# One tile shape for the attention slot's last matmuls, and a planner that counts changes of tile shape

## The chip, the cores and the metric

The kernel runs on one core of one Trainium2 chip. The metric is device time in microseconds (us) of one execution. The kernel before takes 1174.6 us, the median of three runs (1174.29 to 1176.4). The engines are named as the profile names them: PE (TensorE: matmuls; PEld is its weight load), ACT (ScalarE), DVE (VectorE), POOL (GpSimd) and SP (SyncE, which here issues the DMAs). They work at the same time, each through its own list of instructions in order, and wait for each other by semaphores.

## The reference

A masked attention feeds two feed-forward layers. All data are float32.

```
scores = q @ k^T / 8                       # 4 batches x 8 heads, 576 x 576, head size 64
scores = where(scores >= rowmax - tau, scores, -1e9)
attn   = exp(scores - rowmax);  attn = attn / (sum(attn) + 1e-9)
x      = attn @ v                          # heads side by side: 2304 tokens x 512
g  = softplus(x @ w_in);    x = g @ w_out       # layer 1, 512 -> 2048 -> 512
g  = relu(x2 @ w2_in)**2;   out = g @ w2_out    # layer 2, x2 is layer 1's output
```

## The kernel before, in words

**Attention** is cut into 32 units: a group of 288 queries (eight groups, two for each batch) times a pair of heads (four). A unit's scores stand transposed, keys on the 128 partitions and 288 queries along the row. 576 keys are four chunks of 128 and one of 64 for each head; the two 64-key rests of the two heads share the ninth slot of the tile `st` (128 x 9 x 288), head 0's in partitions 0 to 63 and head 1's in 64 to 127. That is the shared slot.

For each unit `a_scores` makes the scores: four chunk pieces (L364), each two matmuls that use 64 of the array's 128 rows, one per head, and a piece for the shared slot (L369). The first eight units multiply in float32; the others split k and q into a high and a low part and make three faster products. ACT copies each result to `st` (L372). `a_max` and `a_soft` take maximum, subtract, mask (DVE, L379 to L405) and exponential (ACT, L406). `a_out` multiplies by v and sums the weights, both in float32: X (head 0 in partitions 0 to 63 of the bank `a_ps0`, head 1 in 64 to 127) takes eight matmuls of 128 rows and 64 columns (L420), D (the sums, in `a_ps1`, head 0 in the upper and head 1 in the lower half) takes eight of 128 rows by the 32 columns of a tile of ones (L427), and the shared slot adds four matmuls to them: X and D for head 0, X and D for head 1 (L432, L433, L432, L433), with 64 rows, and 64 columns for X and 32 for D. ACT copies X and D out, DVE divides.

**Layer 1** has eight groups of 288 tokens and eight steps per group, 64 steps in all: `m1_up` (L463 to L465, three products for the split operands), softplus (ACT L473 to L475, DVE L476), split (`m1_split`: ACT L481, DVE or POOL L482), `m1_down` (L494 to L496). Weights are loaded, split into high and low parts by ACT, DVE and POOL, and stay in SBUF. **Layer 2** follows with five groups of tokens.

**The order** of the instructions on each engine is made by a planner, `Plan`. Every piece of work is added with an engine, a duration in ns, what it reads and writes, and a key (a due time). `emit` schedules them forward in a list simulation, turns the result into new keys by a backward pass, repeats this for 24 rounds, and emits the shortest of the orders. It is called twice: for all attention units with most of layer 1, and for the rest. The banks `a_ps0` and `a_ps1` hold both a unit's scores (from the seventh unit on) and X and D, so that a score piece can start only when ACT has copied the last one out.

Of the kernel before, what the change touches and what calls it, by code (L numbers as in the profile page):

```python
# [2 lines left out]

# [6 lines left out]
F32 = mybir.dt.float32  # L10
# [3 lines left out]
ALU = mybir.AluOpType  # L14
AX = mybir.AxisListType

B, H, S, D = 4, 8, 576, 64
# [9 lines left out]
LAG = 12  # L27
# [10 lines left out]
def f32(ap):  # L38
    return ap.bitcast(F32)


class Plan:
# [3 lines left out]

    SYNC, AFTER_PE, DRAIN, DMA_START, DMA_END, BYTES_PER_NS = 200, 300, 130, 1600, 950, 300

    def __init__(self):
        self.ops, self.writer, self.readers = [], {}, {}
        self.free, self.bus, self.done, self.lock = {}, 0, [], 0

    def add(self, eng, ns, fn, reads=(), writes=(), key=0.0, nbytes=0, lock=False):
        i = len(self.ops)
        deps = set()
        for r in reads:
            if r in self.writer:
                deps.add(self.writer[r])  # L60
            self.readers.setdefault(r, []).append(i)
        for w in writes:
            if w in self.writer:
                deps.add(self.writer[w])
            deps.update(self.readers.pop(w, ()))
            self.writer[w] = i
        deps.discard(i)
        self.ops.append((eng, ns, fn, deps, key, nbytes, lock or eng == "POOL"))

    def emit(self, rounds=24):  # L70

        first, n = len(self.done), len(self.ops)
        state = self.free, self.bus, self.lock
        self.done += [None] * (n - first)
        users = [[] for _ in range(n - first)]
        for i in range(first, n):  # L80
            for d in self.ops[i][3]:
                if d >= first:
                    users[d - first].append(i)
        keys = [op[4] for op in self.ops[first:]]
        best = None
        for r in range(rounds):
            self.free, self.bus, self.lock = dict(state[0]), *state[1:]
            order = self.forward(first, users, keys)
            length = max(self.free.values())
            if best is None or length < best[0]:  # L90
                best = length, order, self.done[first:], (self.free, self.bus, self.lock)
            keys = self.backward(first, users, order)
        _, order, self.done[first:], (self.free, self.bus, self.lock) = best
        for _, _, i in order:
            self.ops[i][2]()

    def forward(self, first, users, keys):
        n = len(self.ops)
        waits = [0] * (n - first)
        ready_at = [0] * (n - first)  # L100
        for i in range(first, n):
            for d in self.ops[i][3]:
                if d < first:
                    ready_at[i - first] = max(ready_at[i - first], self.seen(d, self.ops[i][0]))
                else:
                    waits[i - first] += 1
        engines = sorted({op[0] for op in self.ops[first:]})
        future, ready = {e: [] for e in engines}, {e: [] for e in engines}
        for e in engines:
            self.free.setdefault(e, 0)  # L110

        def release(i):
            heapq.heappush(future[self.ops[i][0]], (ready_at[i - first], keys[i - first], i))

        for i in range(first, n):
            if not waits[i - first]:
                release(i)
        order = []
        while len(order) < n - first:
            best = None  # L120
            for e in engines:
                t = self.free[e]
                if not ready[e] and future[e]:
                    t = max(t, future[e][0][0])
                elif not ready[e]:
                    continue
                if best is None or t < best[0]:
                    best = (t, e)
            t, e = best
            while future[e] and future[e][0][0] <= t:  # L130
                _, key, i = heapq.heappop(future[e])
                heapq.heappush(ready[e], (key, i))
            _, i = heapq.heappop(ready[e])
            eng, ns, fn, deps, key, nbytes, lock = self.ops[i]
            if lock:
                t = max(t, self.lock)
                self.lock = t + ns
            self.free[e] = end = t + ns
            if nbytes:
                self.bus = max(self.bus, t + self.DMA_START) + nbytes / self.BYTES_PER_NS  # L140
                end = self.bus + self.DMA_END
            self.done[i] = (end, e)
            order.append((t, len(order), i))
            for u in users[i - first]:
                ready_at[u - first] = max(ready_at[u - first], self.seen(i, self.ops[u][0]))
                waits[u - first] -= 1
                if not waits[u - first]:
                    release(u)
        return sorted(order)

    def backward(self, first, users, order):
# [18 lines left out]
        while left:  # L170
# [11 lines left out]
                _, key, i = heapq.heappop(future[e])  # L182
                heapq.heappush(ready[e], (key, i))
            _, i = heapq.heappop(ready[e])
            eng, ns, fn, deps, key, nbytes, lock = self.ops[i]
            if lock:
                t = max(t, lock_at)
                lock_at = t + ns
# [29 lines left out]
def kernel(ctx: ExitStack, tc: tile.TileContext, qT, kT, vp, tau, w1i, w1o, w2i, w2o, out):  # L218
# [55 lines left out]
    NX = 5  # L274
    xf_t = many(NX, [128, HALF], "xf")
    w_t = ap.tile([128, 18], F32, name="w_t")
    one_t = ap.tile([128, 32], F32, name="one_t")
    POOL.memset(one_t, 1.0)
    m_d = [dram.tile([18, 32], F32, name=f"m_d{i}") for i in range(4)]


# [4 lines left out]
    class Weights:  # L286
# [7 lines left out]
        def load(self, src, f, outw, key=None, pe=False):  # L294
# [19 lines left out]
            if pe:  # L314
# [6 lines left out]
                b2 = bank if outw else bank.rearrange("p (k f) -> p k f", k=4)  # L321
                P.add("ACT", 530, lambda: ACT.copy(lf, b2), [BK], [W], key)
                return
            P.add("POOL", 1240, lambda: POOL.tensor_tensor(lf, f32(t2), f32(hf), op=ALU.subtract), [T], [W], key)


    def a_load(u, key):
# [10 lines left out]
    def a_prep(u, key):  # L338
        if u < RAW:
            return  # L340
        k_r, q_r, KR, QR = k_rt[u % 2], q_rt[u % 2], ("k_r", u % 2), ("q_r", u % 2)
        P.add("ACT", 330, lambda: ACT.copy(q_h, q_r), [QR], ["q_h"], key)
        P.add("ACT", 630, lambda: ACT.copy(k_h, k_r), [KR], ["k_h"], key)
        P.add("POOL", 750, lambda: POOL.tensor_tensor(q_l, q_r, f32(q_h), op=ALU.subtract), [QR, "q_h"], ["q_l"], key)
        P.add("POOL", 1520, lambda: POOL.tensor_tensor(k_l, k_r, f32(k_h), op=ALU.subtract), [KR, "k_h"], ["k_l"], key)

    def a_scores(u, key):

# [2 lines left out]
        half = [slice(0, 64), slice(64, 128)]  # L351
        ops = [(k_h, q_h), (k_l, q_h), (k_h, q_l)]
        QK = ["k_h", "k_l", "q_h", "q_l"]
        last, ns = 2, [590, 400]
        if u < RAW:
            ops, QK, last, ns = [(k_rt[u % 2], q_rt[u % 2])], [("k_r", u % 2), ("q_r", u % 2)], 0, [590, 590]
        for c in range(5):
            banks = [(y_ps[i], ("y", i)) for i in (2 * (c % 2), 2 * (c % 2) + 1)] if u < EARLY else [(a_ps[i], ("a", i)) for i in range(2)]
            cs = slice(128 * c, 128 * c + 128)
            if c < 4:  # L360
                def mms(banks=banks, cs=cs):
                    for n, (k, q) in enumerate(ops):
                        for o in range(2):
                            PE.matmul(banks[o][0][:, :HALF], k[half[o], cs], q[half[o]], start=(n == 0), stop=(n == last))  # L364
                P.add("PE", ns[0] * cold, mms, QK, [b[1] for b in banks], key + 0.1 * c)
            else:
                def mms(bank=banks[0][0], cs=cs):
                    for n, (k, q) in enumerate(ops):
                        PE.matmul(bank[:, :HALF], k[:, cs], q, start=(n == 0), stop=(n == last))  # L369
                P.add("PE", ns[1] * cold, mms, QK, [banks[0][1]], key + 0.1 * c)  # L370
# [37 lines left out]
    def a_out(u, key):  # L408
# [8 lines left out]
        for c in range(4):  # L417
            def mms(c=c):
                for o in range(2):
                    PE.matmul(X[64 * o:64 * o + 64], vt[:, 256 * o + 64 * c:256 * o + 64 * c + 64], e[:, 5 * o + c], start=(c == 0), stop=False)  # L420
            P.add("PE", (490 + 100 * (c == 0)) * cold, mms, E + [V], [AX0], key)
        for c in range(0, 4, 2):
            def mms(c=c):
                for o in range(2):
                    for i in range(2):
                        a = 64 - 64 * o + 32 * i
                        PE.matmul(D[a:a + 32], one_t, e[:, 5 * o + c + i], start=(c == 0), stop=(c == 2 and i == 1))  # L427
            P.add("PE", (490 + 100 * (c == 0)) * cold, mms, E, [AD], key)

        def mms():  # L430
            for o, h in enumerate(half):
                PE.matmul(X[h], vt[h, 512:], e[h, 4], start=False, stop=True)  # L432
                PE.matmul(D[64 - 64 * o:96 - 64 * o], one_t[h], e[h, 4], start=False, stop=True)  # L433
        P.add("PE", 590 * cold, mms, [E[0], V], [AX0, AD], key)
        P.add("ACT", 310, lambda: ACT.copy(xf, X), [AX0], [XF], key - 0.5)
        for o in range(2):
            P.add("ACT", 310, lambda o=o: ACT.copy(rb[half[o]], D[half[1 - o]]), [AD], [RB], key - 0.5)
# [38 lines left out]
            P.add("DVE", 370, lambda j=j, h=h, a=a: DVE.scalar_tensor_tensor(out=gt_t[j], in0=h, scalar=0.0, in1=a, op0=ALU.max, op1=ALU.add), [("h", j), A], [("gt", j)], key - 0.2)  # L476

    def m1_split(key):
        eng, e, ns = ("POOL", POOL, 750) if key - LAG in GPOOL else ("DVE", DVE, 375)
        for j in range(2):  # L480
            P.add("ACT", 330, lambda j=j: ACT.copy(g_hl[0][j], gt_t[j]), [("gt", j)], [("g_h", j)], key - 0.2)  # L481
            P.add(eng, ns, lambda j=j: e.tensor_tensor(g_hl[1][j], gt_t[j], f32(g_hl[0][j]), op=ALU.subtract), [("gt", j), ("g_h", j)], [("g_l", j)], key - 0.2, lock=True)  # L482
# [211 lines left out]
```

## Time and profile before

| | us |
|---|---|
| median of three runs | 1174.6 |
| profiled execution | 1177.02 |
| its span, first to last instruction | 1175.2 |
| PE busy, share of the span | 1145.8 (98%) |
| DVE busy | 698.6 (59%) |
| ACT busy | 690.8 (59%) |
| POOL busy | 245.6 (21%) |

The span is measured from the first instruction to the last; the 1.8 us between it and the time of that execution lie around it. Busy shares are means over stages that differ: DVE is at 96% of the stretch from 59 to 118 us and at 28% of the last 352 us. Where a row gives "x2" or "x16" that many matmuls are merged into one row; a float32 matmul of the program stands as two MATMUL records in the trace. A tile shape such as 64*32 is rows times columns of the array. A matmul's modelled end lies after the start of the next one, since they are pipelined, so the time of a piece is read from start to start.

### The profile page before, as it was taken

What the parts mean: (1) busy time and instruction counts of PE and PEld (TensorE: products, weight loads), DVE (VectorE), ACT (ScalarE), POOL (GpSimd) and SP (SyncE); (2) the same over time, 40 slices, a digit from 0 to 9 for tenths busy, and PEclk for the clock granted to TensorE, in tenths of its full rate; (3) what the DMA queues carried; (4) which work ended last, traced back from release to release, by engine and by line L of the source; (5) the groups of instructions that cost most, each with busy time, mean ns of one, the idle gap of its engine ahead of it and who ended that gap; (6) DMA issues with size and microseconds to landing.
All of it is one profiled execution on the core that took longest, in us unless ns stands there. A gap on an engine that the chain in (4) does not pass through costs nothing.

```text
span 1175.2 us, 18185 instructions
## 1 busy us (share of the span) xinstructions
PE 1145.8 (98%) x6992; PEld 887.8 (76%) x6992; DVE 698.6 (59%) x992; ACT 690.8 (59%) x1640; POOL 245.6 (21%) x209
## 2 busy tenths in 40 slices
PE   7779999999999999999999999999999999999998
PEld 3335777877877877877777879988888888888887
DVE  5999986766776666657656745889322322222232
ACT  6787887777777776777677657865322222222222
POOL 1024223332332232333223211444000000000000
PEclk9888999999999999999999999999999999999999
DMA  5365422112112112112111004765010010000010
GB/s 190 109 200 181 140 89 84 46 44 81 46 39 83 41 45 83 39 48 74 47 48 42 31 11 146 212 205 159 7 66 1 1 54 1 1 37 1 1 37 19
DMA packets 39291, 81.85 MB, mean 70 GB/s; under 512 B 6180, under 2 KB 14884, under 8 KB 39204
## 3 DMA queue, kind: packets, MB, share of 16 engines
q1 hardware_dynamic: 39204, 80.69, 21.6%
q8 instruction: 55, 0.90, 0.3%
q14 instruction: 32, 0.26, 0.1%
HBM read 71.17 MB, written 9.50 MB: 69 GB/s over the span
## 4 chain that ended last, share of the span: by engine, by line
PE 90%; DVE 4%; ACT 3%; DMA 1%; issue 0%; SPq 0%; ACTq 0%; DVEq 0%
PE h_ps L463 12%; PE h_ps L464 11%; PE h_ps L465 11%; PE y_ps L494 6%; PE y_ps L604 6%; PE y_ps L603 6%; PE y_ps L605 6%; PE y_ps L496 5%; PE y_ps L495 5%; PE a_ps L364 5%; PE a_ps L420 5%; PE a_ps L432 3%; PE a_ps L433 3%; PE a_ps L427 3%; DVE st L402 1%; PE a_ps L369 1%
## 5 line engine op out<-in xcount | busy, mean ns | idle before, releaser
L482 POOL TENSOR_TENSOR g_l<-gt,g_h 128x288 fp32r<-128x288 f32 x96 | 102.8, 1074 | 316.4 <-ACT g_h L481 278.8
L463 PE MATMUL h_ps<-x_h,wih 128*128 128x288 f32 x512 | 160.1, 313 | 0.7 <-DVE gt L476 0.7
L494 PE MATMUL y_ps<-g_h,woh 128*128 128x288 f32 x512 | 158.2, 309 | 0.0
L464 PE MATMUL h_ps<-x_l,wih 128*128 128x288 f32 x512 | 150.5, 294 | 1.2 <-DVE x_l L454 1.2
L465 PE MATMUL h_ps<-x_h,wil 128*128 128x288 f32 x512 | 151.6, 296 | 0.0
L496 PE MATMUL y_ps<-g_l,woh 128*128 128x288 f32 x512 | 151.1, 295 | 0.0
L495 PE MATMUL y_ps<-g_h,wol 128*128 128x288 f32 x512 | 150.9, 295 | 0.0
L402 DVE TENSOR_TENSOR st<-st,mb 64x288 f32<-64x288 f32 (+1 forms) x128 | 129.0, 1022 | 3.3 <-DMA mb<-m_d 2.2
L583 ACT ACTIVATE r<-h_ps 128x512 f32<-128x512 f32 (+1 forms) x80 | 44.5, 556 | 146.2 <-PE h_ps L465 145.8
L584 DVE SCALAR_TENSOR_TENSOR r<-h_ps,r 128x512 f32<-128x512 f32 (+1 forms) x80 | 51.0, 638 | 131.8 <-ACT r L583 131.6
L464 PE MATMUL h_ps<-y_l,wih 128*128 128x512 f32 (+1 forms) x320 | 120.1, 375 | 0.1
L590 ACT CAST g_h<-r 128x512 fp32r<-128x512 f32 (+1 forms) x80 | 46.2, 578 | 125.4 <-PE y_ps L604 125.4
L463 PE MATMUL h_ps<-y_h,wih 128*128 128x512 f32 (+1 forms) x320 | 119.2, 372 | 0.0
L465 PE MATMUL h_ps<-y_h,wil 128*128 128x512 f32 (+1 forms) x320 | 118.7, 371 | 0.0
L591 DVE TENSOR_TENSOR g_l<-r,g_h 128x512 fp32r<-128x512 f32 (+1 forms) x80 | 51.7, 646 | 110.9 <-ACT g_h L590 110.8
L604 PE MATMUL y_ps<-wol,g_h 128*128 128x512 f32 x288 | 114.1, 396 | 0.0
L603 PE MATMUL y_ps<-woh,g_h 128*128 128x512 f32 x288 | 114.1, 396 | 0.0
L605 PE MATMUL y_ps<-woh,g_l 128*128 128x512 f32 x288 | 114.0, 396 | 0.0
L463 PEld LDWEIGHTS h_ps<-x_h,wih 128*128 128x128 f32 x512 | 96.4, 188 | 21.9 <-issue 18.7
L494 PEld LDWEIGHTS y_ps<-g_h,woh 128*128 128x128 f32 x512 | 96.4, 188 | 16.4 <-issue 15.3
L405 DVE SCALAR_TENSOR_TENSOR st<-st,thr 128x1152 f32<-128x1152 f32 (+1 forms) x64 | 104.1, 1628 | 0.1
L476 DVE SCALAR_TENSOR_TENSOR gt<-h_ps,a_t 128x288 f32<-128x288 f32 x128 | 57.4, 450 | 77.3 <-ACT a_t L475 73.9
(102 smaller groups left out, 2410.5 us busy)
## 6 DMA issues: line engine op xcount, KB each, us to landing
k_r<-in_kT SPq DMA_DIRECT2D x32, 320.0 KB
v_t<-in_vp SPq DMA_DIRECT2D x32, 288.0 KB
wraw<-in_w1i SPq DMA_DIRECT2D x16, 512.0 KB
wraw<-in_w1o SPq DMA_DIRECT2D x16, 512.0 KB
wraw<-in_w2i SPq DMA_DIRECT2D x16, 512.0 KB
wraw<-in_w2o SPq DMA_DIRECT2D x16, 512.0 KB
mb<-m_d SPq DMA_DIRECT2D x28, 288.0 KB
q_r<-in_qT SPq DMA_DIRECT2D x32, 144.0 KB
```

Of the source, the lines that this page charges most:

```text
L402: DVE.tensor_tensor(st[p0:p1, a:a + n], st[p0:p1, a:a + n], mb[p0:p1, o:o + 1].to_broadcast([p1 - p0, n, HALF]), op=ALU.subtract),
L405: P.add("DVE", 315 * (s1 - s0), lambda x=x: DVE.scalar_tensor_tensor(out=x, in0=x, scalar=thr, in1=x, op0=ALU.is_lt, op1=ALU.subtract), [] ...
L463: PE.matmul(bank, wih[p][:, c, f], xh[c], start=(c == 0), stop=False)
L464: PE.matmul(bank, wih[p][:, c, f], xl[c], start=False, stop=False)
L465: PE.matmul(bank, wil[p][:, c, f], xh[c], start=False, stop=(c == 3))
L482: P.add(eng, ns, lambda j=j: e.tensor_tensor(g_hl[1][j], gt_t[j], f32(g_hl[0][j]), op=ALU.subtract), [("gt", j), ("g_h", j)], [("g_l", j)] ...
L494: PE.matmul(o, woh[p][:, j, es], g_h[j], start=first, stop=False)
L495: PE.matmul(o, wol[p][:, j, es], g_h[j], start=False, stop=False)
L496: PE.matmul(o, woh[p][:, j, es], g_l[j], start=False, stop=last)
L603: PE.matmul(o, g_h[j][:, ts], woh[p][:, j], start=first, stop=False)
L604: PE.matmul(o, g_h[j][:, ts], wol[p][:, j], start=False, stop=False)
L605: PE.matmul(o, g_l[j][:, ts], woh[p][:, j], start=False, stop=last)
```

## The change

First, the shared slot's four matmuls in `a_out` get one tile shape. The tile of ones grows from 32 to 64 columns, the second half zero, and D's two matmuls use all 64: four tiles of 64 rows by 64 columns, each in its own quarter of the array. D's earlier matmuls keep 32 columns and no longer carry the stop flag. Second, the planner gets a `mode` for each piece on PE (0 is the full array, 1 the chunk scores, 2 X, 3 D, 4 the shared slot), adds 105 ns where the mode changes, and takes a ready piece of the mode that PE is in when its key is within 1000 ns of the first one's. Durations are restated (the shared slot 484 ns where it had 590, chunk scores 393 where they had 590, POOL's subtractions longer). Third, `emit` runs 150 rounds, and every eighth round starts from the best order so far with random shifts of the keys.

```diff
+    SWITCH, NEAR = 105, 1000
-    def emit(self, rounds=24):
+    def emit(self, rounds=150):
-        best = None
+        best, rnd = None, random.Random(1)
...
-            keys = self.backward(first, users, order)
+            keys = self.backward(first, users, order if r % 8 else best[1])
+            if r % 8 == 0 and r:
+                keys = [k + rnd.gauss(0, 1500) for k in keys]
...
-            _, i = heapq.heappop(ready[e])
-            eng, ns, fn, deps, key, nbytes, lock = self.ops[i]
+            key, i = ready[e][0]
+            if e == "PE" and self.ops[i][7] != tiles:
+                key, i = min((r for r in ready[e] if r[0] < key + self.NEAR and self.ops[r[1]][7] == tiles), default=(key, i))
+            ready[e].remove((key, i))
+            heapq.heapify(ready[e])
+            eng, ns, fn, deps, key, nbytes, lock, mode = self.ops[i]
+            if e == "PE" and mode != tiles:
+                ns, tiles = ns + self.SWITCH, mode
...
-    one_t = ap.tile([128, 32], F32, name="one_t")
-    POOL.memset(one_t, 1.0)
+    one_t = ap.tile([128, 64], F32, name="one_t")
+    POOL.memset(one_t, 0.0)
+    POOL.memset(one_t[:, :32], 1.0)
...
-            P.add("POOL", 1240, lambda: POOL.tensor_tensor(lf, f32(t2), f32(hf), op=ALU.subtract), [T], [W], key)
+            P.add("POOL", 1500, lambda: POOL.tensor_tensor(lf, f32(t2), f32(hf), op=ALU.subtract), [T], [W], key)
...
-        last, ns = 2, [590, 400]
+        last, ns = 2, [393, 400]
...
-                        PE.matmul(D[a:a + 32], one_t, e[:, 5 * o + c + i], start=(c == 0), stop=(c == 2 and i == 1))
-            P.add("PE", (490 + 100 * (c == 0)) * cold, mms, E, [AD], key)
+                        PE.matmul(D[a:a + 32], one_t[:, :32], e[:, 5 * o + c + i], start=(c == 0), stop=False)
+            P.add("PE", 484 * cold, mms, E, [AD], key, mode=3)
...
                 PE.matmul(X[h], vt[h, 512:], e[h, 4], start=False, stop=True)
-                PE.matmul(D[64 - 64 * o:96 - 64 * o], one_t[h], e[h, 4], start=False, stop=True)
-        P.add("PE", 590 * cold, mms, [E[0], V], [AX0, AD], key)
+                PE.matmul(D[64 - 64 * o:128 - 64 * o], one_t[h], e[h, 4], start=False, stop=True)
+        P.add("PE", 484 * cold, mms, [E[0], V], [AX0, AD], key, mode=4)
```

All line numbers from L325 on move up by 11 in the changed kernel: L432 and L433 become L443 and L444. What stands on PE at the end of one unit's `a_out`, in the middle of layer 1, before (the two numbers after a name are the tile's own; 32x288 is the output's shape):

```order
L369 MATMUL a_ps_145<-q_l,k_h 128x288
L427 MATMUL a_ps_146<-st_158,one_t 32x288 x8
L420 MATMUL a_ps_145<-st_158,v_t_148 64x288 x8
L432 MATMUL a_ps_145<-st_158,v_t_148 64x288
L433 MATMUL a_ps_146<-st_158,one_t 32x288
L432 MATMUL a_ps_145<-st_158,v_t_148 64x288
L433 MATMUL a_ps_146<-st_158,one_t 32x288
L463 MATMUL h_ps_67<-x_h_125,wih_76 128x288
```

And now, on PE at a like place:

```order
L380 MATMUL a_ps_145<-q_l,k_h 128x288
L438 MATMUL a_ps_146<-st_158,one_t 32x288 x8
L431 MATMUL a_ps_145<-st_158,v_t_148 64x288 x8
L443 MATMUL a_ps_145<-st_158,v_t_148 64x288
L444 MATMUL a_ps_146<-st_158,one_t 64x288
L443 MATMUL a_ps_145<-st_158,v_t_148 64x288
L444 MATMUL a_ps_146<-st_158,one_t 64x288
L505 MATMUL y_ps_63<-g_h_131,woh_90 128x288
```

The order of the slot's four matmuls is the same; D's two are 64 wide now. Over the whole program PE's list holds 464 runs of equal tile shape before and 372 now, so 463 and 371 changes of shape. The slot alone had 96 changes inside it (three in each of 32 units) and has none now; everything else together has 367 before and 371 now.

On PE, two score pieces of one unit with layer 1's matmuls between them, at one of the shortest distances before (nine matmuls; 18 places have nine or eight):

```order
L364 MATMUL a_ps_145<-q_l,k_h 128x288
L364 MATMUL a_ps_146<-q_l,k_h 128x288
L494 MATMUL y_ps_64<-g_h_132,woh_91 128x288
L495 MATMUL y_ps_64<-g_h_132,wol_99 128x288
L496 MATMUL y_ps_64<-g_l_134,woh_91 128x288
L494 MATMUL y_ps_65<-g_h_132,woh_91 128x288
L495 MATMUL y_ps_65<-g_h_132,wol_99 128x288
L496 MATMUL y_ps_65<-g_l_134,woh_91 128x288
L494 MATMUL y_ps_66<-g_h_132,woh_91 128x288
L495 MATMUL y_ps_66<-g_h_132,wol_99 128x288
L496 MATMUL y_ps_66<-g_l_134,woh_91 128x288
L364 MATMUL a_ps_145<-q_h,k_h 128x288
```

And the shortest now (six matmuls; 11 places have six or fewer, 32 have nine):

```order
L375 MATMUL a_ps_145<-q_l,k_h 128x288
L375 MATMUL a_ps_146<-q_l,k_h 128x288
L505 MATMUL y_ps_63<-g_h_132,woh_90 128x288
L506 MATMUL y_ps_63<-g_h_132,wol_98 128x288
L507 MATMUL y_ps_63<-g_l_134,woh_90 128x288
L505 MATMUL y_ps_66<-g_h_132,woh_90 128x288
L506 MATMUL y_ps_66<-g_h_132,wol_98 128x288
L507 MATMUL y_ps_66<-g_l_134,woh_90 128x288
L380 MATMUL a_ps_145<-q_h,k_h 128x288
```

In between ACT must copy two banks out of `a_ps`. On DVE, where the second group of tokens is split for layer 1 (x_l is the low part), before:

```order
L482 TENSOR_TENSOR g_l_134<-gt_138,g_h_132 128x288
L454 TENSOR_TENSOR x_l_127<-xf_175,x_h_123 128x288
L454 TENSOR_TENSOR x_l_128<-xf_171,x_h_124 128x288
L476 SCALAR_TENSOR_TENSOR gt_137<-h_ps_67,a_t_135 128x288
L454 TENSOR_TENSOR x_l_129<-xf_172,x_h_125 128x288
L379 TENSOR_REDUCE m_160<-st_157 128x81
L476 SCALAR_TENSOR_TENSOR gt_138<-h_ps_68,a_t_136 128x288
```

And now, on DVE at the same split:

```order
L390 TENSOR_REDUCE m_160<-st_157 128x81
L451 TENSOR_REDUCE d_168<-rb_166 128x9
L487 SCALAR_TENSOR_TENSOR gt_137<-h_ps_67,a_t_135 128x288
L392 TENSOR_REDUCE m_160<-m_160 128x2x9
L465 TENSOR_TENSOR x_l_127<-xf_175,x_h_123 128x288
L465 TENSOR_TENSOR x_l_128<-xf_171,x_h_124 128x288
L465 TENSOR_TENSOR x_l_129<-xf_172,x_h_125 128x288
```

The first of these x_l is row 216 of DVE's list before and row 219 now, and both orders have all 32 weight slices and seven finished units ahead of it.

## Rows read from the trace of the kernel before

**Rows 1.** The profile's page: busy us (share of the span) and instructions, by engine.

```profile
PE 1145.8 (98%) x6992; PEld 887.8 (76%) x6992; DVE 698.6 (59%) x992; ACT 690.8 (59%) x1640; POOL 245.6 (21%) x209
```

**Rows 2.** Busy time by stretch: stretch, its length, then the engines; clock, DMA, GB/s.

```profile
core 0: us, PE busy (x) PEld busy (x) DVE busy (x) ACT busy (x) POOL busy (x), PEclk, DMA share, GB/s
0.00:31.00 31.00, 20.69 (x66) 11.64 (x66) 18.79 (x22) 21.21 (x56) 3.48 (x11) 0.91 0.55 180
31.00:107.00 76.00, 62.37 (x304) 28.00 (x305) 73.52 (x105) 62.09 (x149) 13.42 (x10) 0.86 0.50 161
107.00:176.00 69.00, 68.52 (x488) 52.47 (x488) 63.21 (x93) 58.85 (x145) 23.34 (x15) 1.00 0.42 128
176.00:235.00 59.00, 58.73 (x421) 45.02 (x423) 42.45 (x60) 43.68 (x112) 18.74 (x16) 1.00 0.20 65
235.00:705.00 470.00, 470.00 (x3446) 361.45 (x3444) 304.88 (x430) 332.94 (x857) 140.93 (x124) 1.00 0.16 50
705.00:1175.20 470.20, 465.53 (x2275) 389.18 (x2273) 195.71 (x285) 172.00 (x325) 45.69 (x34) 1.00 0.18 59
```

**Rows 3.** The chain that ended last, by engine, from the page.

```profile
PE 90%; DVE 4%; ACT 3%; DMA 1%; issue 0%; SPq 0%; ACTq 0%; DVEq 0%
```

**Rows 4.** PE's timeline at one unit's output: start, length, line, tiles, shape, count.

```profile
400.69 0.29 PE L496 MATMUL y_ps<-g_l,woh 128*128 128x288 f32 x1
400.92 2.16 PE L420 MATMUL a_ps<-st,v_t 128*64 128x288 f32 x16
403.01 0.69 PE L432 MATMUL a_ps<-st,v_t 64*64 64x288 f32 x2
403.64 0.67 PE L433 MATMUL a_ps<-st,one_t 64*32 64x288 f32 x2
404.24 0.70 PE L432 MATMUL a_ps<-st,v_t 64*64 64x288 f32 x2
404.86 0.67 PE L433 MATMUL a_ps<-st,one_t 64*32 64x288 f32 x2
405.46 0.40 PE L494 MATMUL y_ps<-g_h,woh 128*128 128x288 f32 x1
```

**Rows 5.** PE's shared-slot matmuls by shape, from 176 to 705 us.

```profile
L432 PE MATMUL a_ps<-st,v_t 64*64 64x288 f32 x100 | 34.8, 428 | 0.0
L433 PE MATMUL a_ps<-st,one_t 64*32 64x288 f32 x98 | 32.8, 415 | 0.0
```

**Rows 6.** PE's timeline at an early unit's output.

```profile
46.19 1.18 PE L427 MATMUL a_ps<-st,one_t 128*32 128x288 f32 x16
47.29 0.70 PE L432 MATMUL a_ps<-st,v_t 64*64 64x288 f32 x2
```

**Rows 7.** PE's timeline around one chunk score piece.

```profile
409.01 0.29 PE L465 MATMUL h_ps<-x_h,wil 128*128 128x288 f32 x1
409.23 0.40 PE L364 MATMUL a_ps<-q_h,k_h 64*128 64x288 f32 x2
409.47 0.29 PE L364 MATMUL a_ps<-q_h,k_l 64*128 64x288 f32 x2
409.60 0.29 PE L364 MATMUL a_ps<-q_l,k_h 64*128 64x288 f32 x2
409.82 0.40 PE L463 MATMUL h_ps<-x_h,wih 128*128 128x288 f32 x1
410.06 0.29 PE L464 MATMUL h_ps<-x_l,wih 128*128 128x288 f32 x1
410.19 0.29 PE L465 MATMUL h_ps<-x_h,wil 128*128 128x288 f32 x1
```

**Rows 8.** PE's timeline: the end of a score piece and the start of the next.

```profile
431.53 0.29 PE L364 MATMUL a_ps<-q_l,k_h 64*128 64x288 f32 x2
...
433.55 0.40 PE L364 MATMUL a_ps<-q_h,k_h 64*128 64x288 f32 x2
```

**Rows 9.** ACT's timeline at the copies of these two score pieces.

```profile
409.99 0.69 ACT L372 ACTIVATE st<-a_ps 128x288 f32<-128x288 f32 x2
...
430.49 1.50 ACT L406 ACTIVATE st<-st,qsc 128x1440 f32<-128x1440 f32 x1
431.89 0.39 ACT L473 ACTIVATE a_t<-h_ps 128x288 f32<-128x288 f32 x1
432.18 0.70 ACT L372 ACTIVATE st<-a_ps 128x288 f32<-128x288 f32 x2
```

**Rows 10.** POOL's one instruction on the tile of ones: ns, and its start in us.

```profile
L278 POOL MEMSET one_t<- x1: 114/114/114, 1.4 to 1.4; 128x32 f32 x1
```

**Rows 11.** DVE's timeline at the second group's split.

```profile
175.04 0.82 DVE L482 TENSOR_TENSOR g_l<-gt,g_h 128x288 fp32r<-128x288 f32 x2
175.78 0.82 DVE L454 TENSOR_TENSOR x_l<-xf,x_h 128x288 fp32r<-128x288 f32 x2
```

More of the change, by code (lines that the diff above doesn't have):

```diff
@@ L1 @@
 import heapq
+import random
 from contextlib import ExitStack
@@ L53, in __init__, with add @@
         self.free, self.bus, self.done, self.lock = {}, 0, [], 0
-    def add(self, eng, ns, fn, reads=(), writes=(), key=0.0, nbytes=0, lock=False):
+    def add(self, eng, ns, fn, reads=(), writes=(), key=0.0, nbytes=0, lock=False, mode=0):
         i = len(self.ops)
@@ L67, in add @@
         deps.discard(i)
-        self.ops.append((eng, ns, fn, deps, key, nbytes, lock or eng == "POOL"))
-    def emit(self, rounds=24):
+        self.ops.append((eng, ns, fn, deps, key, nbytes, lock or eng == "POOL", mode))
+    def emit(self, rounds=150):
         first, n = len(self.done), len(self.ops)
@@ L117, in forward @@
                 release(i)
-        order = []
+        order, tiles = [], 0
         while len(order) < n - first:
@@ L184, in backward @@
             _, i = heapq.heappop(ready[e])
-            eng, ns, fn, deps, key, nbytes, lock = self.ops[i]
+            eng, ns, fn, deps, key, nbytes, lock, mode = self.ops[i]
             if lock:
@@ L343, in a_prep @@
         P.add("ACT", 630, lambda: ACT.copy(k_h, k_r), [KR], ["k_h"], key)
-        P.add("POOL", 750, lambda: POOL.tensor_tensor(q_l, q_r, f32(q_h), op=ALU.subtract), [QR, "q_h"], ["q_l"], key)
-        P.add("POOL", 1520, lambda: POOL.tensor_tensor(k_l, k_r, f32(k_h), op=ALU.subtract), [KR, "k_h"], ["k_l"], key)
+        P.add("POOL", 1000, lambda: POOL.tensor_tensor(q_l, q_r, f32(q_h), op=ALU.subtract), [QR, "q_h"], ["q_l"], key)
+        P.add("POOL", 1630, lambda: POOL.tensor_tensor(k_l, k_r, f32(k_h), op=ALU.subtract), [KR, "k_h"], ["k_l"], key)
     def a_scores(u, key):
@@ L353, in a_scores @@
         QK = ["k_h", "k_l", "q_h", "q_l"]
-        last, ns = 2, [590, 400]
+        last, ns = 2, [393, 400]
         if u < RAW:
-            ops, QK, last, ns = [(k_rt[u % 2], q_rt[u % 2])], [("k_r", u % 2), ("q_r", u % 2)], 0, [590, 590]
+            ops, QK, last, ns = [(k_rt[u % 2], q_rt[u % 2])], [("k_r", u % 2), ("q_r", u % 2)], 0, [484, 484]
         for c in range(5):
@@ L364, in mms @@
                             PE.matmul(banks[o][0][:, :HALF], k[half[o], cs], q[half[o]], start=(n == 0), stop=(n == last))
-                P.add("PE", ns[0] * cold, mms, QK, [b[1] for b in banks], key + 0.1 * c)
+                P.add("PE", ns[0] * cold, mms, QK, [b[1] for b in banks], key + 0.1 * c, mode=1)
             else:
@@ L420, in mms @@
                     PE.matmul(X[64 * o:64 * o + 64], vt[:, 256 * o + 64 * c:256 * o + 64 * c + 64], e[:, 5 * o + c], start=(c == 0), stop=False)
-            P.add("PE", (490 + 100 * (c == 0)) * cold, mms, E + [V], [AX0], key)
+            P.add("PE", 484 * cold, mms, E + [V], [AX0], key, mode=2)
         for c in range(0, 4, 2):
@@ L478, in m1_split @@
     def m1_split(key):
-        eng, e, ns = ("POOL", POOL, 750) if key - LAG in GPOOL else ("DVE", DVE, 375)
+        eng, e, ns = ("POOL", POOL, 1000) if key - LAG in GPOOL else ("DVE", DVE, 375)
         for j in range(2):
```

## The prediction

> **What bounds the kernel now.** I read the page's busy times first, then the busy times by stretch, the chain of waits, PE's timeline at single units, and ACT's at the same moments. The reader is to see that PE is busy for 98% of the span [rows 1] and that 90% of the chain that ended last is PE's [rows 3]. A busy PE need not be a limiting one, since the modelled ends of its matmuls overlap; so the timelines decide. From 235 to 705 us PE is busy for all of 470 us at a granted clock of 1.00, which is 2.4 GHz, while DVE has 65% and ACT 71% [rows 2]; at a unit's output the next piece starts as soon as the one before lets it [rows 4]. In that stretch what is taken from PE is taken from the time. Before 176 us it is otherwise. From 31 to 107 us DVE is busy for 73.52 of 76 us and PE for 62.37 at a clock of 0.86: DVE is the limit and PE waits. From 107 to 176 us both are near theirs, PE with 68.52 and DVE with 63.21 of 69 us [rows 2]. The profiled execution took 1177.0 us and its span 1175.2, so 1.8 us lie around it; the median of the runs is 1174.6. I work out differences on the span and take them from the median.
>
> **The shared slot's matmuls, the large term.** At one unit the four pieces start at 403.01, 403.64, 404.24 and 404.86, and the next work at 405.46: 2.45 us, in four turns of 0.60 to 0.63 us [rows 4]. Each turn is one float32 matmul alone, with a change of tile shape ahead of it. The new piece has one shape, and its four matmuls use four different quarters of the array. Do they run at once? D's earlier matmuls show four column tiles doing so: sixteen records in 47.29 - 46.19 = 1.10 us [rows 6], where the slot needs 2.45 us for eight. The chunk scores show two row tiles doing so: three pairs take 409.82 - 409.23 = 0.59 us [rows 7], and three single full matmuls take 0.39 to 0.40 (0.13 each, 410.06 to 410.19). The trace shows no row and column tiles together. The bounds for the new piece are therefore 0.60 us, one turn, and 2.45 us, no gain; less than one turn is excluded, since one float32 matmul must pass. I take 0.63, the turn with 64 columns, because row tiles and column tiles each overlap fully where they stand alone. That is 2.45 - 0.63 = 1.82 us per unit. From 176 to 705 us the trace has 100 records of L432, four per unit: 25 units [rows 5] (98 of the other line; two records are missing). 25 x 1.82 = 45.5 us, all on the path.
>
> Row against rule: the two matmuls of X write the same bank from different row tiles, and so do D's, though to different partitions. In the scores the two row tiles write to two banks [rows 7]. No row shows two row tiles in one bank. The Trainium skill, "TensorEngine Tiling (Array Packing)", Restrictions and Gotchas, Gotcha 1, says that different row tiles cannot access the same PSUM bank at the same time. By that rule the slot's two heads would go one after the other; what this gives is the first rival below. No run so far shows whether the rule holds for separate partitions.
>
> **The first seven units** (32 less 25) end before 176 us. PE waits for DVE up to 107 us, so what PE saves there turns into waiting: nothing. From 107 to 176 us three units' outputs lie; the bounds are 0 and 3 x 1.82 = 5.5 us. DVE is then the limit: its 63.21 us at the share it reached from 31 to 107 us (96.7%) take 65.4 us, so 69 - 65.4 = 3.6 us can be had. I take 3.6, near the upper end, because DVE has shown this share for 76 us.
>
> **The new order.** Outside the slot PE changes its tile shape 371 times instead of 367, so the rule that keeps like pieces together wins nothing here. What a change costs: from 409.01 to 410.06 there are five turns of 0.13 us, 0.66 us, and two changes; 1.05 - 0.66 = 0.39 us, 0.195 each [rows 7]. Four more cost 0.8 us.
>
> Between two score pieces of one unit ACT must copy two banks. Without a hold-up the second copy ends at 409.99 + 0.69 = 410.68, 1.08 us after the last score started at 409.60 [rows 7, 9]. Behind an Exp that began at 430.49 and one short operation it ends at 432.88, 1.35 us after 431.53 [rows 8, 9]. With twelve matmuls in between, PE came back after 433.55 - 431.53 = 2.02 us [rows 8]; with six it would come back after 2.02 - 6 x 0.13 = 1.24 us. That is 0.16 us more than 1.08 and 0.11 us less than 1.35, so 11 such places cost from nothing to some 3 us, if the Exp begins late. I take 2 us. Behind a waiting score piece stands all of layer 1's work on PE, so it is lost in full.
>
> DVE's list has the second group's split, which came at 175.78 us [rows 11], three rows later. A DVE instruction took 63.21 / 93 = 0.68 us from 107 to 176 us [rows 2]; three are 2.0 us, on DVE's path, from nothing to 2.
>
> The rounds and restarts act through the orders alone, which are counted above. What else they move: POOL's list keeps its work, with one more fill of the tile of ones (114 ns at 1.4 us [rows 10], where a unit's output needs its scores and exponentials first), and POOL is busy for 21% [rows 1]. SP's loads stand in a slightly other order; DMA takes 0.42 of its time from 107 to 176 us and 0.16 later [rows 2], so a load that moves by a piece is covered. If that cover were gone, a weight load would hold the early, DVE-bound stage, where 2 us are already allowed. Layer 2, after 705 us, is untouched: 465.53 of 470.20 us are PE.
>
> Sum: 45.5 + 3.6 - 0.8 - 2.0 - 2.0 = 44.3 us. The span would be 1130.9 us and the median 1174.6 - 44.3 = 1130.3; I say 1130.
>
> **Rivals.** (1) The two heads of the slot go one after the other. The second pair adds 0.49 us (X's sixteen records, two at a time, take 403.01 - 400.92 = 2.09 us for four float32 matmul times and one change of shape, so at most 0.52 for each [rows 4]; less the change, 0.49). The piece is 1.12 us, the gain 1.33 per unit, 12.2 us less over 25 units: 1142.5. For it: one bank from two row tiles is new. Against: the partitions differ, and column tiles in one bank run together [rows 6].
>
> (2) The early stage gains as well, because the restarts find an order in which DVE's idle 2.48 us from 31 to 107 us and 12.2 us before 31 us [rows 2] shrink. If all seven early units' 12.7 us come through instead of 3.6, and the 2.0 us of DVE don't count: 1130.3 - 11.1 = 1119. Against: DVE is at 97% there, and its work is the same.
>
> (3) PE loses half of the gain to layer 1's own chain, in which ACT and DVE stand between up and down projection: 1174.6 - 22 = 1152. Against: in the long stretch ACT has 71% [rows 2], and would have 470 / (470 - 22 x 1.82) x 71% = 78%.
>
> (4) Slower. ACT takes its work in order, and a 1.50 us Exp [rows 9] just ahead of the two copies makes PE wait at the next score piece: 1.50 + 0.69 - 1.24 = 0.95 us at a distance of six matmuls. 25 units have 100 such reuses of the banks. The loss passes the gain from 44.3 / 0.95 = 47 hits on, half of them; with 70 hits it is 66 us, and the time 1196. For it: places at such short distance are more (11 at six, none before). Against: only these 11 are that short, and at the distances of before PE is idle for 0.00 of 470 us [rows 2].
>
> **How the numbers follow.** My forecast has 0.72, with a range of its own of 1124 (no cost of the order, 5.5 early) to 1137; rival 1 has 0.13, rival 2 0.07, rival 3 0.05, rival 4 0.03. The range that should hold the time 8 times in 10 reaches into rivals 1 and 2: 1117 to 1145. A measurement of this kernel tells about 0.2%, 2.3 us, from no change. Rivals 1 to 3 and the forecast are faster: 0.72 + 0.13 + 0.07 + 0.05 = 0.97, of which I move 0.01 to no change. So 0.96 faster, 0.01 the same, 0.03 slower.
>
> **What would show it.** In the changed kernel's PE timeline the slot's four lines start within hundredths of a us of each other, and the next piece 0.6 us after them; 1.1 us would be rival 1. The second group's split on DVE should come near 174 us, with more idle PE before it. After it PE should be without idle time, and the score pieces should wait for ACT's copies for about 2 us in all; tens of us there would be rival 4. If PE is idle for more than 10 us after 200 us, the forecast's step "all on the path" is wrong.

## The result, and the profile after

The changed kernel takes 1130.2 us (median of four runs, 1128.7 to 1132.6) where the kernel before takes 1175.5; the ratio is 0.9614, with an interval from 0.9590 to 0.9638. The forecast was 1130, inside a range of 1117 to 1145. The profiled execution took 1129.8 us, its span 1128.1, 47.1 us less than before. PE is busy for 1090.8 us instead of 1145.8 [rows 1], still nearly all of the span; the page's row of busy times:

```profile
PE 1090.8 (97%) x6992; PEld 871.4 (77%) x6992; DVE 680.1 (60%) x992; ACT 685.2 (61%) x1640; POOL 244.5 (22%) x210
```

PE's timeline at one unit's output, to be set beside [rows 4] (start, length, line, tiles, shape, count):

```profile
396.19 2.16 PE L431 MATMUL a_ps<-st,v_t 128*64 128x288 f32 x16
398.28 0.45 PE L443 MATMUL a_ps<-st,v_t 64*64 64x288 f32 x1
398.29 0.45 PE L444 MATMUL a_ps<-st,one_t 64*64 64x288 f32 x1
398.29 0.45 PE L443 MATMUL a_ps<-st,v_t 64*64 64x288 f32 x1
398.30 0.45 PE L444 MATMUL a_ps<-st,one_t 64*64 64x288 f32 x1
398.57 0.40 PE L443 MATMUL a_ps<-st,v_t 64*64 64x288 f32 x1
398.58 0.40 PE L444 MATMUL a_ps<-st,one_t 64*64 64x288 f32 x1
398.59 0.40 PE L443 MATMUL a_ps<-st,v_t 64*64 64x288 f32 x1
398.59 0.40 PE L444 MATMUL a_ps<-st,one_t 64*64 64x288 f32 x1
398.93 0.40 PE L505 MATMUL y_ps<-g_h,woh 128*128 128x288 f32 x1
```

The four matmuls of the slot, each two records, start within 0.02 us of each other, twice, and the next work follows 0.65 us after the first (398.93 - 398.28). Before, the piece took 2.45 us. The busy times by stretch, to be set beside [rows 2]:

```profile
0.00:31.00 31.00, 18.98 (x69) 9.75 (x71) 19.52 (x22) 21.25 (x56) 3.61 (x12) 0.82 0.55 180
31.00:107.00 76.00, 60.01 (x311) 26.14 (x307) 71.63 (x102) 61.57 (x149) 15.49 (x10) 0.78 0.49 160
107.00:176.00 69.00, 65.39 (x499) 52.01 (x498) 62.68 (x97) 61.43 (x148) 26.81 (x19) 1.00 0.45 131
176.00:235.00 59.00, 59.00 (x472) 48.87 (x472) 47.03 (x68) 46.43 (x123) 16.85 (x15) 1.00 0.22 65
235.00:660.00 425.00, 424.77 (x3374) 347.94 (x3372) 295.08 (x423) 326.45 (x847) 134.52 (x124) 1.00 0.18 55
```

The early stretches look much as they did: DVE is busy for 94% of the time from 31 to 107 us, and PE waits more than before and at a lower granted clock (0.78 where it was 0.86). From 107 to 176 us PE now has 3.6 us without work where it had 0.5. From 176 to 660 us it has 0.2 us of that. From 176 to 705 us the slot's line has 96 records where it had 100 [rows 5], 24 units:

```profile
L443 PE MATMUL a_ps<-st,v_t 64*64 64x288 f32 x96 | 17.0, 428 | 0.0
```

The eighth unit's slot starts at 172.88 us, ahead of that mark; before the change it started at 178.01 us, behind it.

### The profile page after: what moved, and what is told of

Its sections match the earlier page's. It is cut to its first block, busy times and chain, and to the rows that moved or that the text cites. A ratio compares the mean times of both kernels' runs of the same rounds, so it can differ in the third digit from the quotient of the medians.

```text
span 1128.1 us, 18169 instructions
## 1 busy us (share of the span) xinstructions
PE 1090.8 (97%) x6992; PEld 871.4 (77%) x6992; DVE 680.1 (60%) x992; ACT 685.2 (61%) x1640; POOL 244.5 (22%) x210
## 4 chain that ended last, share of the span: by engine, by line
PE 91%; DVE 4%; ACT 4%; issue 1%; DMA 0%; SPq 0%; DVEq 0%
PE h_ps L474 13%; PE h_ps L476 12%; PE h_ps L475 12%; PE y_ps L505 7%; PE y_ps L614 6%; PE y_ps L615 6%; PE y_ps L616 6%; PE y_ps L507 6%; PE y_ps L506 6%; PE a_ps L375 5%; PE a_ps L431 5%; PE a_ps L438 3%; PE a_ps L443 2%; DVE m L390 1%; ACT st L383 1%; PE a_ps L380 1%
## 5 line engine op out<-in xcount | busy, mean ns | idle before, releaser
L594 ACT ACTIVATE r<-h_ps 128x512 f32<-128x512 f32 (+1 forms) x80 | 44.3, 555 | 157.6 <-PE h_ps L476 155.6
L413 DVE TENSOR_TENSOR st<-st,mb 128x1152 f32<-128x1152 f32 (+1 forms) x128 | 126.7, 1004 | 1.8 <-DMA mb<-m_d 0.9
```

Of the source, the lines that this page charges most:

```text
L413: DVE.tensor_tensor(st[p0:p1, a:a + n], st[p0:p1, a:a + n], mb[p0:p1, o:o + 1].to_broadcast([p1 - p0, n, HALF]), op=ALU.subtract),
```

## The experiments

All ratios are to the kernel before, run beside the experiment on the same chip. There are three groups: the first four below; then the first three of the planner's parts and the first kernel with an output as one piece; then the two seeds and the last two kernels. The kernel before took 1175.6, 1176.5 and 1176.3 us beside them. Differences are taken between medians. The changed kernel's 1130.2 us was measured apart from all three groups (beside 1175.5 us), so a difference to it, or between groups, is known to some 2 to 3 us only, by the intervals of the ratios. In the edits "..." marks lines left out.

**The shape without the order.** The kernel before, its planner untouched, with

```diff
-    one_t = ap.tile([128, 32], F32, name="one_t")
-    POOL.memset(one_t, 1.0)
+    one_t = ap.tile([128, 64], F32, name="one_t")
+    POOL.memset(one_t, 0.0)
+    POOL.memset(one_t[:, :32], 1.0)
...
-                PE.matmul(D[64 - 64 * o:96 - 64 * o], one_t[h], e[h, 4], start=False, stop=True)
+                PE.matmul(D[64 - 64 * o:128 - 64 * o], one_t[h], e[h, 4], start=False, stop=True)
```

D's earlier matmuls take the first 32 columns and lose the stop flag, as in the changed kernel.

> The kernel before, with its planner and its order untouched, and only the shared slot's four matmuls in one shape (64 ones columns, the second half zero). Theory 1 (PE's time from about 200 us on is the kernel's time, and the new order is worth little): 24 or 25 units x 1.80 us and some 4 us from the stretch before, so 1175.5 - 47 = 1127 to 1132 us. Rival (the planner's restarts and its rule on tile shapes brought a good part of the 45 us): 1140 us or more.

Measured: 1126.3 us, ratio 0.9581 (0.9568 to 0.9594); 49.3 us less than before, and 0.7 us under the range of theory 1. The rival falls. The time is 3.9 us under the changed kernel's, at the edge of what the two intervals tell apart: the shape brought the whole gain, and probably more than that.

**The order without the shape.** The changed kernel with the edits above undone.

> The changed kernel's order of instructions, word for word the changed planner, but the shared slot's matmuls in the old two shapes (D with 32 columns). Theory 1 (the order alone is worth little): 1171 to 1178 us. Rival (the order brought a good part): 1165 us or less.

Measured: 1181.6 us, ratio 1.0047 (1.0033 to 1.0061): slower, by 6.0 us. The rival falls; the time is above what theory 1 expected as well. Together the four kernels make a square: the shape takes 49.3 us off the old order and 1181.6 - 1130.2 = 51.4 off the new one, and the new order adds 6.0 us to the old shape and 3.9 to the new one (51.4 and 3.9 are differences to the changed kernel). Within what can be told apart, the two add up.

Where the order's time goes: two rows of the stretch from 107 to 123 us, of the kernel before and of this one (PE, PEld, DVE, ACT, POOL, clock, DMA, GB/s).

```profile
107.00:123.00 16.00, 16.00 (x105) 12.88 (x103) 16.00 (x17) 13.84 (x35) 9.38 (x6) 1.00 0.50 154
```

```profile
107.00:123.00 16.00, 12.42 (x71) 9.01 (x69) 13.39 (x24) 14.46 (x36) 4.61 (x4) 0.89 0.53 167
```

PE loses 3.6 us there, and the granted clock is lower too, 0.89; the changed kernel loses as much in this stretch (12.39 of 16 us busy) at a clock of 1.00. The timeline of PE in the second kernel says what ended each idle stretch (in brackets):

```profile
109.77 0.76 PE L374 MATMUL a_ps<-q_r,k_r 64*128 64x288 f32 x4 [1.14 <-ACT st L382]
111.33 0.76 PE L374 MATMUL a_ps<-q_r,k_r 64*128 64x288 f32 x4 [0.81 <-ACT st L382]
118.16 0.75 PE L379 MATMUL a_ps<-q_r,k_r 128*128 128x288 f32 x2 [0.49 <-ACT st L382]
120.87 0.68 PE L437 MATMUL a_ps<-st,one_t 128*32 128x288 f32 x4 [0.37 <-ACT st L382]
122.31 0.68 PE L437 MATMUL a_ps<-st,one_t 128*32 128x288 f32 x4 [0.76 <-ACT st L416]
```

These are score pieces and an output that stand in PE's list too soon after the last ones, so that PE waits for ACT to copy or to finish an exponential. The changed kernel has the same waits there, 1.6 to 3.1 us earlier. Over the whole span PE is without work for 35.0 us in this kernel and for 29.4 us before: 1.9 us more up to 107 us, 3.1 more from 107 to 176, 0.7 more after 660. So this place is more than half of the order's cost. The order also starts layer 1 one output later. Of its first matmul line, before and in this kernel (ns at least, median and most; first and last start):

```profile
L463 PE MATMUL h_ps<-x_h,wih x512: 292/297/606, 89.4 to 761.5; 128*128 128x288 f32 x171
```

```profile
L473 PE MATMUL h_ps<-x_h,wih x512: 292/297/442, 102.7 to 773.5; 128*128 128x288 f32 x171
```

In the changed kernel layer 1 starts at 101.0 us.

**Which units count.** The changed kernel, the old shapes in the slot for `u < 8` only.

> The changed kernel, with the old two shapes in the shared slot of the first eight units and the new shape in the other 24. Theory 1 (up to about 176 us DVE is the limit, and what PE saves there turns into waiting): 0 to 4 us above the changed kernel, 1130 to 1134 us. Rival (PE's time counts there too): 8 x 1.80 = 14.4 us above it, 1144.5 us.

Measured: 1138.0 us, ratio 0.9680 (0.9667 to 0.9694). Against the run of the order without the shape, of the same group, the 24 later units gain 1181.6 - 1138.0 = 43.6 us, 1.82 for each: what the piece itself lost (2.45 - 0.65 = 1.80). The first eight gain 1138.0 - 1130.2 = 7.8 us, 0.98 for each, between my 0 to 4 and the rival's 14.4. By the two intervals the 7.8 may be 4.5 to 11. So some of what PE saves in the early stage comes through, and DVE is not its only limit.

**Two tiles at once.** The changed kernel, with X of both heads and then D of both heads, D 32 wide.

```diff
...
             for o, h in enumerate(half):
                 PE.matmul(X[h], vt[h, 512:], e[h, 4], start=False, stop=True)
-                PE.matmul(D[64 - 64 * o:128 - 64 * o], one_t[h], e[h, 4], start=False, stop=True)
+            for o, h in enumerate(half):
+                PE.matmul(D[64 - 64 * o:96 - 64 * o], one_t[h, :32], e[h, 4], start=False, stop=True)
```

> The changed kernel, with the slot's four matmuls as two pairs, X of both heads (64 columns) and then D of both heads (32 columns): one change of shape inside, two tiles at once instead of four. Theory 1 (a turn of matmuls costs 0.60 to 0.63 us with its change, and each turn more counts in some 24 units): the piece takes 1.23 us instead of 0.645, 24 x 0.585 = 14 us more, 1144 us. Rival (what the old shapes cost is the change of shape alone, 0.2 us each): 24 x 0.2 = 5 us more, 1135 us.

Measured: 1146.5 us, ratio 0.9752 (0.9739 to 0.9766), 16.3 us above the changed kernel. Its PE timeline:

```profile
406.04 0.70 PE L443 MATMUL a_ps<-st,v_t 64*64 64x288 f32 x4
406.67 0.68 PE L445 MATMUL a_ps<-st,one_t 64*32 64x288 f32 x4
407.28 0.40 PE L506 MATMUL y_ps<-g_h,woh 128*128 128x288 f32 x1
```

The piece takes 1.24 us, 0.59 more; 24 units make 14.2, and the first eight the rest (at most 4.7). The rival falls. What the old shapes cost is turns: each turn more takes 0.6 us, and a change of shape, 0.195 us by [rows 7], is the smaller part of it. The two heads of X, two row tiles in one bank, run in one turn here too (406.67 - 406.04 = 0.63 us).

**The planner's parts.** Three kernels take one part of the changed kernel's planner back, two have another seed.

```diff
-    SWITCH, NEAR = 105, 1000
+    SWITCH, NEAR = 0, 0
```

> The changed kernel, but the planner adds nothing for a change of tile shape and does not look for a like piece (both constants 0); the restated durations and the restarts stay. Its PE order has 427 changes of shape instead of 371, and starts layer 1 after the fourth unit's output, as before, instead of after the fifth. Theory 1 (each change costs 0.195 us of PE's time, and PE's time is the kernel's from about 180 us on): 56 x 0.195 = 10.9 us more, less up to 4 us of the late start, 1137 to 1141 us. Rival (the changes don't matter, the rule's cost to the order does): 1124 to 1128 us.

Measured: 1144.7 us, ratio 0.9726 (0.9711 to 0.9740), 14.5 above the changed kernel and 3.7 above theory 1's range; more than the 11 us of its 56 changes of shape. Its order loses time elsewhere too: from 176 to 235 us PE is without work for 1.6 us, at a granted clock of 0.97, where the changed kernel has none and 1.00. The rival falls: with the restated durations the rule is needed. My reading, not shown, is that these took out what the old durations had in them for a change of shape (590 ns for a chunk score piece, now 393), and that the rule puts it back.

```diff
-    def emit(self, rounds=150):
+    def emit(self, rounds=24):
...
-            keys = self.backward(first, users, order if r % 8 else best[1])
-            if r % 8 == 0 and r:
-                keys = [k + rnd.gauss(0, 1500) for k in keys]
+            keys = self.backward(first, users, order)
```

> The changed kernel with 24 rounds and no random shifts; the tile rule and the restated durations stay. 364 changes of shape instead of 371; layer 1 starts after the fourth unit's output. Theory 1 (what the new order costs lies before 200 us: the restarts chose an order that starts layer 1 one output later): 1130.2 - 1.4 - up to 3 = 1125 to 1129 us. Rival (the restarts help, as more search finds a shorter order): 1132 us or more.

Measured: 1131.7 us, ratio 0.9620 (0.9607 to 0.9633), 1.5 above the changed kernel. Theory 1 fails here: this order starts layer 1 after the fourth output (at 93.2 us), and is no faster for it. Whether the restarts help is not shown either: 1.5 us are within what can be told apart.

```diff
-            P.add("POOL", 1500, ...
+            P.add("POOL", 1240, ...
-        last, ns = 2, [393, 400]
+        last, ns = 2, [590, 400]
...
```

> The changed kernel with the durations of before in the planner for POOL's subtractions and for PE's attention pieces; the tile rule and the restarts stay. 385 changes of shape instead of 371; layer 1 starts after the fourth unit's output. Theory 1: 14 x 0.195 = 2.7 us more, less up to 4 us, 1129 to 1133 us. Rival (the restated durations make the order better): 1134 us or more.

Measured: 1133.8 us, ratio 0.9644 (0.9631 to 0.9657), at the border of the two theories: 3.6 us more, hardly clear of the changed kernel, of which 14 changes of shape make 2.7.

```diff
-        best, rnd = None, random.Random(1)
+        best, rnd = None, random.Random(2)   # and 3
```

> The changed kernel with another seed for the planner's random shifts (2 instead of 1), nothing else: another order, with 368 changes of tile shape instead of 371. Theory 2 (what the new order costs against the old is no one rule's doing but differs from order to order, in idle time and low clock before 200 us): 1124 to 1134 us, off the changed kernel by more than the 0.6 us of three changes. Rival (restated durations and rule cost a fixed 4 us): 1129 to 1131 us.

> The changed kernel with the third seed, 366 changes of shape. Theory 2: 1124 to 1134 us, and not the time of seed 2. Rival (fixed cost): 1128 to 1130 us, as seeds 1 and 2.

Measured: 1132.4 us (1130.7 to 1133.5) and 1129.3 us (1127.8 to 1132.9), ratios 0.9622 and 0.9595. With seed 1's 1130.2 the three overlap. Seed 2 lies 1.4 us above its rival's range and seed 3 inside its own, and neither is clear of the changed kernel, so the runs do not decide between theory 2 and a fixed cost. All three medians lie above the 1126.3 of the old planner, but the interval of seed 3 overlaps that one's. Which part of the new planner costs the 4 us stays open.

**A unit's output as one piece.** The old planner with the slot's one shape, and X, D and slot added as one piece on PE:

```diff
...
-            P.add("PE", (490 + 100 * (c == 0)) * cold, mms, E + [V], [AX0], key)
+            parts.append(mms)
...
-        P.add("PE", 590 * cold, mms, [E[0], V], [AX0, AD], key)
+        parts.append(mms)
+        P.add("PE", 3730 * cold, lambda: [f() for f in parts], E + [V], [AX0, AD], key)
```

> The kernel before with the shared slot's one shape (as in the first of these runs, 1126.3 us) and a unit's whole output, X, D and slot, as one piece on PE, so that nothing comes in between: 346 changes of shape instead of 367. Layer 1 starts after the fifth output. Theory 1: 21 x 0.195 = 4.1 us less, and up to 4 us more at the start: 1122 to 1126 us. Rival (a piece of 3.7 us holds up layer 1's up and down projection behind it, so that ACT, DVE and then PE wait): 1130 us or more.

Measured: 1132.0 us, ratio 0.9623 (0.9610 to 0.9636): 5.7 us slower than the same without the piece. The gain of 21 changes is lost, and more. Two places show in its trace: layer 1 starts at 104.3 us (87.9 without the piece), and after 200 us PE waits once for POOL, the rival's kind of wait:

```profile
PE y_ps L499 <- POOL g_l L485: 2.7, 1, 2.7
```

What each of the two costs was not separated. The same from the ninth unit on alone, with the early order free of it:

```diff
-            parts.append(mms)
+            if u < 8:
+                P.add("PE", (490 + 100 * (c == 0)) * cold, mms, E + [V], [AX0], key)
+            else:
+                parts.append(mms)
...
```

> The old planner with the slot's one shape, and from the ninth unit on a unit's output as one piece: 355 changes of shape where the same without the piece has 367 (1126.3 us); layer 1 starts after the fourth output. Theory 1: 12 x 0.195 = 2.3 us less, 1124 us, if the start is as good; by theory 2 the start may be off by 3 us either way: 1121 to 1127 us. Rival (long pieces on PE hold up layer 1, as the whole-program piece with 1132.0 us may have shown): 1130 us or more, with PE idle after 200 us.

Measured: 1124.5 us (1122.2 to 1126.1), ratio 0.9555 (0.9540 to 0.9570), as theory 1 had it; the rival falls. And the changed kernel with the same edit (the piece is given 3800 ns) and another price for a change of shape:

```diff
-    SWITCH, NEAR = 105, 1000
+    SWITCH, NEAR = 195, 1000
```

> The changed planner with 195 ns for a change of shape instead of 105 (what the trace shows), and a unit's output as one piece from the ninth unit on: 355 changes instead of 371. Theory 1: 16 x 0.195 = 3.1 us less than 1130.2, 1127 us, and by theory 2 within 3 us of it: 1124 to 1130 us. Rival (long pieces hold up layer 1): 1133 us or more.

Measured: 1122.3 us (1121.6 to 1122.6), ratio 0.9537 (0.9524 to 0.9550): the fastest of all, 7.9 us under the changed kernel, below the whole range expected, and 4 under the shape alone. Against the old planner with the same piece, of the same group, it is 2.2 us less, and the times of the two just overlap; that the new planner is the better one is not shown. Its stretches:

```profile
31.00:107.00 76.00, 57.30 (x320) 27.20 (x319) 74.18 (x106) 63.04 (x154) 19.19 (x11) 0.81 0.52 163
107.00:176.00 69.00, 67.95 (x522) 55.73 (x520) 62.93 (x96) 61.86 (x151) 28.97 (x18) 0.99 0.41 129
176.00:235.00 59.00, 59.00 (x477) 47.64 (x477) 49.23 (x66) 47.13 (x122) 19.11 (x16) 1.00 0.22 69
235.00:660.00 425.00, 424.46 (x3399) 350.42 (x3398) 300.33 (x430) 326.45 (x850) 134.73 (x122) 1.00 0.18 53
```

DVE is fuller from 31 to 107 us than in the changed kernel (74.18 against 71.63), PE loses only 1 us from 107 to 176, and the number of matmul records is higher in every stretch shown. Sixteen changes of shape fewer are 3.1 us; the other 4.8 us I put down to the better start. Layer 1's first matmul stands at 87.3 us here, as with the shape alone (87.9), and at 101.0 us in the changed kernel. That an early first matmul is enough is not so: the kernel with the old durations has it at 86.2 us and takes 1133.8. Whether the 195 or the piece brought the better start was not separated.

## Why the prediction was right, step by step

**The slot's piece** was put at 0.63 us and is 0.65. That four quarters of the array run at once was not in the trace before; it was put together from column tiles and row tiles seen apart, and held. Rival 1, which had the two heads one after the other, falls with the timeline (its 0.49 us for the second pair should have been (2.09 - 0.195) / 4 = 0.47, which moves its time by 0.4 us): both heads of X write the bank `a_ps0`, at 398.28 and 398.29 us. The rule cited for it, Gotcha 1 of the Trainium skill's "TensorEngine Tiling (Array Packing)", Restrictions and Gotchas, does not hold here in its wide form: these two row tiles start 0.01 us apart in one bank, in different partitions, and the whole piece takes 0.65 us. Another page of the Trainium skill, "PSUM — Partial Sum Buffer", under "PSUM bank collisions raise a hardware error", reports the collision of two row tiles for one bank and one quadrant of 32 partitions; this kernel's tiles never share a quadrant, and no run here tried that.

**25 units on the path.** The later 24 units count in full, 1.82 us each, by the run that leaves the old shapes in the first eight. The term of 45.5 us is 43.6 for 24 units; the eighth moved to the early side. "All on the path" held.

**The early units** were put at 3.6 us for those between 107 and 176 us, 5.4 with the eighth counted in full; the first eight bring 7.8, with 4.5 to 11 possible. The reason given was that DVE would tighten to the share it had before. In the changed kernel it did not: DVE has 62.68 of 69 us from 107 to 176 us, as before (63.21). With the shape alone, in the old order, it did, and went beyond the 96.7%, to 98%:

```profile
107.00:176.00 69.00, 68.02 (x517) 53.73 (x516) 67.55 (x100) 62.72 (x154) 25.11 (x18) 1.00 0.43 131
```

So the reason held for the shape in the old order, and did not show in the new one, which has 3.6 us of idle PE there. Up to 107 us I put the gain at nothing; the runs do not separate that part. A shorter output also shortens the chain from an output to the next step, which I left out; that this chain brings the rest is my reading, not shown.

**The order's cost** was put at 4.8 us and is 6.0 without the shape (3.9 to 7.2 by the interval of the ratio) and 3.9 with it. The size was right and the places only in part. The four changes of shape are there. The score pieces at six matmuls' distance, which I charged 2 us, cost almost nothing: after 200 us PE was idle for these reasons,

```profile
PE h_ps L474 <- DVE gt L487: 1.7, 1, 1.7
PE a_ps L375 <- ACT st L383: 0.2, 1, 0.2
```

0.2 us in all for ACT's copies. The waits came earlier, from 107 to 123 us, where the first eight units' slower float32 scores stand. The start of layer 1 one output later, at 101.0 us where it was 89.4, is not in the prediction; what it costs by itself is open, since the order of 24 rounds starts layer 1 at 93.2 us and is no faster. The second group's split on DVE was to come near 174 us and came at 177.47:

```profile
177.47 1.18 DVE L465 TENSOR_TENSOR x_l<-xf,x_h 128x288 fp32r<-128x288 f32 x3
```

So the forecast's closeness to 0.2 us owes something to luck. By the runs the shape gave 43.6 + 7.8 = 51.4 us where I had 49.1, and the order took 6.0 where I had 4.8: 1.0 us more gain than the 44.3 forecast. The kernel before took 1175.5 us beside the changed one, 0.9 more than the 1174.6 I subtracted from, and the two cancel.

**Rival 2** has part of its size, by the first eight units' 7.8 us, and not its mechanism: DVE's idle time from 31 to 107 us grew from 2.5 to 4.4 us. **Rival 3** would be PE idle after 200 us: it is 1.9 us there by the rows above. **Rival 4** had the right kind of wait, score pieces behind ACT, but far more of it than there is.

## What to carry to other kernels

Where PE is the limit, small matmuls that each use a part of the array should stand next to each other in one tile shape and in different parts; here widening an operand with zeros, which does more arithmetic, took 1.8 us off each unit's piece. A planner is worth testing by itself, with the rest of the change taken out: here the hand-made shape gave all of the gain and the new order took some of it back. Giving the planner the price that the trace shows (0.195 us for a change of shape) and keeping a unit's output together from the ninth unit on brought the fastest kernel; which of the two did it was not separated. Where another engine limits a stage, do not put what PE saves there at nothing: here about half of it came through (0.98 of 1.8 us for each unit).

## What the runs showed of the hardware

Four tiles of 64 x 64, two of them in each of two banks, ran at once with float32 data: 0.65 us for the four, where one alone had taken 0.60 to 0.63. A change of tile shape costs PE 0.195 us on average by the rows before; the kernel with 56 changes more took 14.5 us more, which would be 0.26 us each if nothing else had moved. PE's granted clock from 31 to 107 us was 0.86 before and 0.78 in the changed kernel, a mean of stretches at 2.4 GHz (1.00) and at 1.2, and 1.00 from 107 to 176 us in both. Over the experiments it does not simply follow PE's idle time: the shape alone has PE busy for 57.36 us from 31 to 107 us at 0.85, the changed kernel for 60.01 at 0.78.
